# Two tuned MoE layers on one core: where finished sums are emptied, and a further block whose matmuls use 64-row tiles

## The chip, the cores and the metric

One core of a Trainium2 chip. The metric is the device time of one execution in microseconds (us): the median of three executions, beside one profiled execution whose trace is read here.

## What is computed

A causal 7-tap convolution with softmaxed weights of its own for every token, then two feed-forward layers of width 2048, each with its own activation:

```
w = softmax(weight_gen)                    # 8192 tokens, 8 heads, 7 taps
x = sum over k of w[..., k] * x_pad[t + k]  # 192 channels
h = x @ w_in;   g = h if h >= 1, 0 if h <= -1, else (h + 1)**2 / 4;   x = g @ w_out      # layer 1
h = x @ w_in2;  g = h - tanh(h);                                      out = g @ w_out2   # layer 2
```

## The kernel before, in words

**Blocks and items.** The 8192 tokens are 16 blocks of 512, the 2048 hidden units 16 groups of 128. An item (m, b, f) is layer m (0 and 1 in the code, layers 1 and 2 in the words), block b, group f. It has a first product into one PSUM bank (`ps6`, `ps7`, `ps1`, `ps0` in turn), an activation, and a second product that adds to the block's two sum banks (`ps2`, `ps3` in layer 1; `ps4`, `ps5` in layer 2 from block 1 on). Each float32 operand is split into a rounded part and a rest, and the products are taken of the parts. So an item has these operations between its two products: in layer 1 ACT L795 and L796, DVE L797, ACT L801 (`gh`, the rounded part), DVE L805 (`gl`, the rest); in layer 2 ACT L799, DVE L800, then L801 and L805 alike. `g` has 3 buffers, `gh` and `gl` have 4.

**Order of the blocks.** From the sixth block on layers take turns: layer 1 of block 3, layer 2 of block 2, layer 1 of block 4, layer 2 of block 3, and so on to layer 1 of block 15, layer 2 of block 14 and last layer 2 of block 15.

**Two modes of TensorE.** In 128-row mode (`mm1`, L781, and L817 to L824) an item is 5 + 5 matmuls of 512 columns, one after another. In 64-row mode two half-height matmuls run beside each other, the low lane and the high lane; the 192 inputs of a block then need no padding, and an item is 19 half-height matmuls, 9.5 for each lane. `paired(m, b)` (L641) says which blocks use it. There the plan takes two items f, f+1 as a pair of 19 steps, in three pieces (`both`, L720): `one` (9 steps), `two` and `three` (5 each). Piece `three` of a pair holds the low half of the second product of the even item of the pair before; piece `two` that of the odd item of two pairs before; high halves follow later. A sum is therefore complete only in the third pair of the next block (`done`, L714).

**Beside them.** The convolution of a later block: 0.95 us operations on DVE (L445, L492, L581, L576, L584), paced by `turn` (L385). It ends in two 32 by 32 transposes (L576) whose rows go to DRAM and come back as the next layer-1 block's input (`move_rows`, DMAs L596, L603 to L607). And the emptying of a finished sum: `finish1` (layer 1: ACT L856, DVE L858, ACT L853, DVE L857, ACT L859, DVE L860, and the copy `x3` L865 that 64-row mode needs) and `finish2` (layer 2: ACT L886, DVE L887, L888, L889, then 24 stores L884).

**What sets the order.** A list scheduler at build time (`Plan.run`): each task has a key, the item at which it is due, and each modelled engine takes the ready task with the smallest key. It only fixes the order in which each engine's instructions stand. On the chip each engine works its list in that order, and an instruction waits for the data it needs, holding up all behind it on its engine.

Of the kernel before, what the change touches and what calls it, by code (L numbers as in the profile page):

```python
# [23 lines left out]
MOVED = 4  # L24
# [133 lines left out]
def on(engine, dur):  # L158
    return {engine: (dur, 0.0)}
# [3 lines left out]
def tile_dynconv_moe_moe(  # L163
# [17 lines left out]
    NB = NT // N  # L181
    NF = FF // P
    D1 = D - P
# [46 lines left out]
    def x3(s):  # L230

        n, k = divmod(s.n, 2)
        if n not in x3_t:
            x3_t[n] = const.tile([P, 2, N], F32R, tag=f"raw{n}", name=f"x3_{n}")
        return x3_t[n][D1:P, k]
# [14 lines left out]
    plan = Plan()  # L250
# [23 lines left out]
    order = []  # L274
# [10 lines left out]
    marks = {}  # L285
# [81 lines left out]
    xdone = {}  # L367
    a_of, b_of, x3_of = {}, {}, {}
    x3_free = []

    def conv(b, banks, base, gap):
# [7 lines left out]
        count, paced = [0], [0.0]  # L379
# [5 lines left out]
        def turn(k):  # L385

            if b < MOVED:
                return []
            paced[0] += k
            n = int(base + PACE * paced[0])  # L390
            return [marks["gl", it] for it in [order[n]] if n < at[0, b, 0] and ("gl", it) in marks]

        def load_wg(e):
# [38 lines left out]
        t = plan.add(on("DVE", 0.30), key(), lambda e: e.tensor_reduce(MX(), W(), axis=AX.X, op=ALU.max), [lw] + turn(0.5), takes=soft, uses=[wg], own=0.12 if early else 0.0)  # L432
        t = plan.add(on("DVE", 0.30), key(), lambda e: e.tensor_tensor(W(), W(), bc(MX()), op=ALU.subtract), [t] + turn(0.5), uses=[wg] + soft, lock=not early)
# [51 lines left out]
        tasks, sums = [], []  # L485
# [152 lines left out]

    def paired(m, b):

        return b >= MOVED - m and (m, b) != (1, NB - 1)  # L641

    def lanes1(i):

# [69 lines left out]
    def done(g, t):  # L714

        if g in late2 and late2[g][2] == NF - 1:
            m, b, f, *_, acc, need = late2[g]
            (finish1 if m == 0 else finish2)(b, acc, g + (9.0 if m == 0 else 11.0), t)

    def both(m, b, f, h0, h1, need):  # L720

# [46 lines left out]
    def item(m, b, f, after):  # L768
# [36 lines left out]
        tlo = plan.add(engines, i, lambda e: e.tensor_tensor(GL(), G_(), GH().bitcast(F32), op=ALU.subtract), [thi], takes=[gl], uses=[g], lock=True)  # L805

        marks["gl", (m, b, f)] = tlo
        w = wout[m][:, f, :]
        a, z = f == 0, f == NF - 1
        need = [wdone.get((1, m, f // 2)), prev2.get((m, b))]  # L810
# [31 lines left out]
            (finish1 if m == 0 else finish2 if b < NB - 1 else finish_last)(b, acc, i + LAG + 0.6, t)  # L842
        return first

    def finish1(b, acc, key, t):
        s, tm = slot("xt"), slot("val")
        b_of[b] = s
        X, M = lambda k: xt_t[s.n][:, k], lambda: vals[tm.n][0:D1]
        p0, p1 = lambda: ps[acc[0].n], lambda: ps[acc[1].n]

        def hi(e):
            xt_tile(s, f"b_{b}")
            e.copy(X(0), p0())  # L853

        h0 = plan.add(on("ACT", 0.60), key, hi, [t], takes=[s], uses=acc)
        h1 = plan.add(on("ACT", 0.60), key, lambda e: e.copy(M(), p1()[D1:P]), [t], takes=[tm], uses=acc)  # L856
        l0 = plan.add(on("DVE", 0.60), key, lambda e: e.tensor_tensor(X(1), p0(), X(0).bitcast(F32), op=ALU.subtract), [h0], uses=acc + [s])  # L857
        r = plan.add(on("DVE", 0.60), key, lambda e: e.tensor_tensor(M(), p1()[0:D1], M(), op=ALU.add), [h1], uses=acc + [tm])  # L858
        rh = plan.add(on("ACT", 0.525), key, lambda e: e.copy(X(2)[0:D1], M()), [r], uses=[s, tm])  # L859
        rl = plan.add(on("DVE", 0.60), key, lambda e: e.tensor_tensor(X(2)[D1:P], M(), X(2)[0:D1].bitcast(F32), op=ALU.subtract), [rh], uses=[s, tm])  # L860
        marks["fin1", b] = r
        xdone[1, b] = [h0, l0, rh, rl]
        if paired(1, b):
            s3 = x3_of[1, b] = slot("x3")
            xdone[1, b].append(plan.add(on("ACT", 0.525), key, lambda e: e.copy(x3(s3), M()), [r] + x3_free, takes=[s3], uses=[tm]))  # L865

    def out_raws():

        return (0, 1)

    def finish2(b, acc, key, t):

        s, tm = slot("raw", out_raws), slot("val")
        R = lambda: raws[s.n].rearrange("p a b -> p (a b)").bitcast(F32)
        M = lambda: vals[tm.n][0:D1]
        p0, p1 = lambda: ps[acc[0].n], lambda: ps[acc[1].n]

        def store(e, c):
            r = R()[c * 32:(c + 1) * 32, 0:N] if c < P // 32 else R()[c * 32 - P:c * 32 - P + 32, N:]
            r = r.rearrange("p (u v c) -> p u v c", u=T, c=32)  # L880
            for n in range(T):

                o = out_sq[:, :, b * T + n, c * 32:(c + 1) * 32]
                e.dma_start(o, r[:, :, n] if b >= MOVED else r[:, n])  # L884

        h1 = plan.add(on("ACT", 0.60), key, lambda e: e.copy(M(), p1()[D1:P]), [t], takes=[tm], uses=acc)  # L886
        t0 = plan.add(on("DVE", 0.60), key, lambda e: e.transpose(R()[:, 0:N], p0()), [t], takes=[s], uses=acc)  # L887
        r = plan.add(on("DVE", 0.60), key, lambda e: e.tensor_tensor(M(), p1()[0:D1], M(), op=ALU.add), [h1], uses=acc + [tm])  # L888
        t1 = plan.add(on("DVE", 0.60), key, lambda e: e.transpose(R()[0:D1, N:], M()), [r, t0], uses=[s, tm])  # L889
        for c in range(D // 32):  # L890
            plan.add(on("DMA", 2.6), key, lambda e, c=c: store(e, c), [t0 if c < P // 32 else t1], uses=[s], late=3.0)

# [29 lines left out]
    for n, (m, b) in enumerate(streams):  # L922
# [5 lines left out]
        for f in range(NF):  # L928
# [9 lines left out]
            if (m, b, f) == (1, NB - 2, NF - 1):  # L938
                close(at[m, b, f] + 1)

    tasks = plan.run()
    with tc.manual_schedule():
        for t in tasks:
# [41 lines left out]
```

## Time and profile before

| | before |
|---|---|
| runs | 1181.68, 1182.35, 1183.67 us, median 1182.35 |
| the profiled execution | 1182.38 us, of which the span from first to last instruction is 1180.6 us |
| PE | 1144.8 us busy, 97% of the span |
| DVE, ACT, POOL | 995.9 (84%), 849.1 (72%), 94.0 us (8%) |
| granted TensorE clock | mean 0.995 of full speed; under nine tenths in the second of 40 slices alone |
| DMA | 60.5 MB, 51 GB/s over the span |

An engine's busy time is the union of its instructions. A matmul's end is modelled, so short gaps between matmuls hardly show in PE's busy time; the distance between the starts of two matmuls shows them.

### The profile page before, as it was taken

The page shows a single profiled execution, that of the slowest core. Times are in us where ns is not written, and L with a number is a line of the kernel's source. Part 1 is how long each engine was busy: PE and PEld are TensorE (multiplying, and loading weights), DVE is VectorE, ACT ScalarE, POOL GpSimd, SP SyncE. Part 2 cuts the span into 40 slices and gives each one's busy share as a digit, 9 for nine tenths or more (in the row PEclk, how much of TensorE's full clock was granted, in tenths as well). Part 3 has the DMA queues.
Part 4 walks back from the last instruction along what each step waited for, and adds up shares of the span by engine and source line. Part 5 has one row for each costly group of instructions (what it writes and reads, how often), then busy time and mean ns, then how long its engine had stood idle before and what let it go on. Part 6 is the DMA issues. An engine that isn't in the chain of part 4 may idle for free.

```text
span 1180.6 us, 23472 instructions
## 1 busy us (share of the span) xinstructions
PE 1144.8 (97%) x8648; PEld 1027.2 (87%) x8648; DVE 995.9 (84%) x1523; ACT 849.1 (72%) x1511; POOL 94.0 (8%) x81
## 2 busy tenths in 40 slices
PE   3899999999999999999999999999999999999998
PEld 2677888888998998889989888999989999999987
DVE  8998998887988879898888989889888888976665
ACT  4989996675867767677676867767686676767653
POOL 4744451000000000000000000000000000000000
PEclk9899999999999999999999999999999999999999
DMA  6522130211130301203021130301213020110000
GB/s 206 161 71 79 54 121 8 52 50 48 19 92 13 89 11 32 79 15 96 9 53 51 19 92 15 96 4 33 76 19 92 12 62 1 27 47 15 1 10 19
DMA packets 93034, 60.50 MB, mean 51 GB/s; under 512 B 56060, under 2 KB 81274, under 8 KB 92920
## 3 DMA queue, kind: packets, MB, share of 16 engines
q1 hardware_dynamic: 92732, 58.62, 18.1%
q8 instruction: 68, 1.11, 0.4%
q10 hardware_dynamic: 188, 0.39, 0.1%
q14 instruction: 46, 0.38, 0.1%
HBM read 43.24 MB, written 15.73 MB: 50 GB/s over the span
## 4 chain that ended last, share of the span: by engine, by line
PE 87%; ACT 6%; DVE 4%; issue 1%; POOL 1%; DMA 1%; DVEq 0%; ACTq 0%
PE ps L677 36%; PE ps L693 31%; PE ps L781 10%; PE ps L823 2%; PE ps L824 2%; PE ps L817 2%; PE ps L818 2%; PE ps L819 2%; ACT g L795 1%; ACT g L796 1%; ACT gh L801 1%; PE ps L834 1%; DVE gl L805 1%; DVE raw L887 1%; ACT val L886 1%
## 5 line engine op out<-in xcount | busy, mean ns | idle before, releaser
L677 PE MATMUL ps<-gh,wout 64*128 64x512 f32 x2304 | 731.9, 387 | 0.0
L677 PE MATMUL ps<-gl,wout 64*128 64x512 f32 x1536 | 597.8, 389 | 3.2 <-DVE gl L805 3.1
L677 PEld LDWEIGHTS ps<-gh,wout 64*128 64x128 f32 x2304 | 421.8, 184 | 26.4 <-ACT gh L801 0.3
L693 PE MATMUL ps<-a,win 64*128 64x512 f32 x1632 | 408.7, 389 | 0.0
L693 PE MATMUL ps<-b,win 64*128 64x512 f32 x1632 | 403.1, 387 | 0.0
L801 ACT CAST gh<-g 128x512 fp32r<-128x512 f32 x512 | 314.3, 617 | 105.1 <-PE ps L677 40.6
L805 DVE TENSOR_TENSOR gl<-g,gh 128x512 fp32r<-128x512 f32 x476 | 327.5, 692 | 41.4 <-ACT gh L801 26.2
L693 PEld LDWEIGHTS ps<-a,win 64*128 64x128 f32 x1632 | 298.1, 184 | 14.4 <-issue 0.4
L693 PEld LDWEIGHTS ps<-b,win 64*128 64x128 f32 x1632 | 300.2, 184 | 5.6
L677 PEld LDWEIGHTS ps<-gl,wout 64*128 64x128 f32 x1536 | 282.7, 184 | 19.7 <-DVE gl L805 12.1
L799 ACT ACTIVATE g<-ps 128x512 f32<-128x512 f32 x256 | 152.8, 598 | 132.6 <-PE ps L693 115.0
L800 DVE TENSOR_TENSOR g<-ps,g 128x512 f32<-128x512 f32 x256 | 174.0, 686 | 67.7 <-ACT g L799 66.5
L797 DVE SCALAR_TENSOR_TENSOR g<-ps,g 128x512 f32<-128x512 f32 x256 | 174.6, 685 | 47.5 <-ACT g L796 44.8
L795 ACT ACTIVATE g<-ps 128x512 f32<-128x512 f32 x256 | 151.5, 592 | 53.5 <-PE ps L693 38.7
L796 ACT ACTIVATE g<-g 128x512 f32<-128x512 f32 x256 | 161.9, 632 | 6.5
L781 PE MATMUL ps<-a,win 128*128 128x512 f32 x320 | 88.0, 411 | 6.2 <-POOL win L351 3.1
L781 PE MATMUL ps<-b,win 128*128 128x512 f32 x320 | 83.3, 391 | 0.0
L781 PEld LDWEIGHTS ps<-a,win 128*128 128x128 f32 x320 | 62.7, 198 | 23.4 <-POOL win L351 4.3
L445 DVE TENSOR_TENSOR prod<-xw,wg 128x768 f32<-128x768 f32 x84 | 80.9, 963 | 0.0
L693 PE MATMUL ps<-x,win 64*128 64x512 f32 x192 | 74.3, 387 | 0.0
L781 PEld LDWEIGHTS ps<-b,win 128*128 128x128 f32 x320 | 59.1, 188 | 12.0 <-issue 0.4
L492 DVE TENSOR_TENSOR acc<-acc,prod 128x768 f32<-128x768 f32 x70 | 67.4, 963 | 0.0
(89 smaller groups left out, 890.4 us busy)
## 6 DMA issues: line engine op xcount, KB each, us to landing
xw<-in_x_dram SPq DMA_DIRECT2D x14, 960.0 KB, 7.0
spot<-xw SPq DMA_DIRECT2D x96, 96.0 KB, 2.0
raw<-in_moe_w_out_dram SPq DMA_DIRECT2D x16, 384.0 KB, 3.1
a<-spot SPq DMA_DIRECT2D x24, 256.0 KB, 3.3
out_dram<-raw SPq DMA_DIRECT2D x360, 16.0 KB, 1.5
raw<-in_moe_w_in_dram SPq DMA_DIRECT2D x16, 256.0 KB, 3.4
raw<-in_moe_w_in_dram SPq DMA_DIRECT2D x32, 128.0 KB, 3.4
a<-spot SPq DMA_DIRECT2D x24, 128.0 KB, 3.3
```

The lines of the kernel that those rows point to most:

```text
L445: e.tensor_tensor(dst.rearrange("p j (h g) -> p j h g", h=H), xws[xw.n][:, k:k + T, :].rearrange("p j (h g) -> p j h g", h=H), w[:, :, :, ...
L492: e.tensor_tensor(prods[k % 2] if early and k == mine - 1 else acc_sb, acc_sb, prods[k % 2], op=ALU.add)
L677: return e.matmul(to(), w[rs, c:c + P], (GL() if low else GH())[rs], start=f == 0 and lane == 0 and n == 0, stop=f == NF - 1 and lane == 1 ...
L693: return e.matmul(ps[h.n], win[m][rs, k, fs], x, start=lane == 0 and n == 0, stop=lane == 1 and n == len(ops) - 1)
L781: e.matmul(ps[h.n], w[:, k, fs], xt[:, c], start=n == 0, stop=n == 4)
L795: t = plan.add(on("ACT", 0.60), i, lambda e: e.activation(G_(), H_(), AF.Relu, bias=0.5, scale=0.5), [first], takes=[g], uses=[h], late=0.1)
L796: t = plan.add(on("ACT", 0.537), i, lambda e: e.activation(G_(), G_(), AF.Square), [t], uses=[g])
L797: t = plan.add(on("DVE", 0.605), i, lambda e: e.scalar_tensor_tensor(G_(), H_(), 1.0, G_(), op0=ALU.max, op1=ALU.min), [t], uses=[g, h])
L799: t = plan.add(on("ACT", 0.49), i, lambda e: e.activation(G_(), H_(), AF.Tanh), [first], takes=[g], uses=[h])
L800: t = plan.add(on("DVE", 0.605), i, lambda e: e.tensor_tensor(G_(), H_(), G_(), op=ALU.subtract), [t], uses=[g, h])
L801: thi = plan.add(on("ACT", 0.527), i, lambda e: e.copy(GH(), G_()), [t], takes=[gh], uses=[g])
L805: tlo = plan.add(engines, i, lambda e: e.tensor_tensor(GL(), G_(), GH().bitcast(F32), op=ALU.subtract), [thi], takes=[gl], uses=[g], lock= ...
```

## The change

Three edits.

1. The emptying of a sum in 64-row mode gets dependences in the plan alone (`held`): each of its ACT and DVE operations stands behind `gh` or `gl` of a certain later item. If g is the last item of the block, so that g + 4 is f = 3 of the next block, then the copy of half a sum stands behind `gh` of f = 3, and the other operations behind `gh` or `gl` of f = 4, 5 and 6.
2. `turn` skips f = 3 to 6 when it paces the convolution of blocks 4 to 15.
3. `paired` takes in layer 2 of block 2: 16 more items in 64-row mode. Its block then needs an `x3` copy (13 of them now instead of 12), and this copy now reads the rounded part in `b` and not `val`.

```diff
-            paced[0] += k
-            n = int(base + PACE * paced[0])
+            paced[0] += k * PACE
+            while int(base + paced[0]) % NF in (3, 4, 5, 6):
+                paced[0] += 1.0
+            n = int(base + paced[0])
...
-        return b >= MOVED - m and (m, b) != (1, NB - 1)
+        return b >= MOVED - 2 * m and (m, b) != (1, NB - 1)
...
-            (finish1 if m == 0 else finish2)(b, acc, g + (9.0 if m == 0 else 11.0), t)
+            (finish1 if m == 0 else finish2)(b, acc, g + (9.0 if m == 0 else 11.0), t, g)
...
+    held = []
+    def hold(g, tasks):
+        if g is not None:
+            held.extend((t, kind, g + n) for t, kind, n in tasks)
...
+        hold(g, [(h1, "gh", 4), (r, "gl", 5), (h0, "gh", 5), (l0, "gl", 6), (rh, "gh", 6), (rl, "gl", 7)])
...
-            xdone[1, b].append(plan.add(on("ACT", 0.525), key, lambda e: e.copy(x3(s3), M()), [r] + x3_free, takes=[s3], uses=[tm]))
+            xdone[1, b].append(plan.add(on("ACT", 0.525), key, lambda e: e.copy(x3(s3), X(2)[0:D1]), [rh] + x3_free, takes=[s3], uses=[s]))
...
+        hold(g, [(h1, "gh", 4), (r, "gl", 5), (t0, "gl", 6), (t1, "gl", 7)])
...
+    for t, kind, n in held:
+        t.deps.append(marks[kind, order[n]])
```

In the changed kernel every line from L389 on stands 2 or more lines later: L797 is L799 there, L805 L807, L445 L447, L492 L494, L677 L679, L693 L695, L781 L783, and L887, L888, L889 are L898, L899, L900.

DVE, from the third item of a layer-1 block on (block 5; the same in blocks 4 to 14). `g` written from a `ps` bank is the activation of the next item (f = 2, 3, then 4, 5, 6, 7), `gl` the rest of the items in the same order, `raw` and `val` the emptying, `prod` and `acc` the convolution. Before:

```order
L797 SCALAR_TENSOR_TENSOR g2_97<-ps1_66,g2_97 128x512
L797 SCALAR_TENSOR_TENSOR g0_95<-ps0_65,g0_95 128x512
L887 STREAM_TRANSPOSE raw0_85<-ps4_64 128x512
L805 TENSOR_TENSOR gl0_102<-g2_97,gh3_101 128x512
L805 TENSOR_TENSOR gl2_104<-g0_95,gh0_98 128x512
L445 TENSOR_TENSOR prod0_94<-xw1_92,wg1_78 128x768
L797 SCALAR_TENSOR_TENSOR g1_96<-ps6_67,g1_96 128x512
L888 TENSOR_TENSOR val0_89<-ps4_64,val0_89 64x512
L889 STREAM_TRANSPOSE raw0_85<-val0_89 64x512
L805 TENSOR_TENSOR gl1_103<-g1_96,gh1_99 128x512
L797 SCALAR_TENSOR_TENSOR g2_97<-ps7_68,g2_97 128x512
L492 TENSOR_TENSOR acc0_93<-acc0_93,prod0_94 128x768
```

And in the change:

```order
L799 SCALAR_TENSOR_TENSOR g2_97<-ps1_66,g2_97 128x512
L799 SCALAR_TENSOR_TENSOR g0_95<-ps0_65,g0_95 128x512
L807 TENSOR_TENSOR gl0_102<-g2_97,gh3_101 128x512
L807 TENSOR_TENSOR gl2_104<-g0_95,gh0_98 128x512
L799 SCALAR_TENSOR_TENSOR g1_96<-ps6_67,g1_96 128x512
L799 SCALAR_TENSOR_TENSOR g2_97<-ps7_68,g2_97 128x512
L807 TENSOR_TENSOR gl1_103<-g1_96,gh1_99 128x512
L899 TENSOR_TENSOR val0_89<-ps4_64,val0_89 64x512
L807 TENSOR_TENSOR gl3_105<-g2_97,gh2_100 128x512
L898 STREAM_TRANSPOSE raw0_85<-ps4_64 128x512
L799 SCALAR_TENSOR_TENSOR g0_95<-ps1_66,g0_95 128x512
L799 SCALAR_TENSOR_TENSOR g1_96<-ps0_65,g1_96 128x512
```

Before, the transpose of the sum stood ahead of `gl` of f = 2 and 3, and convolution operations stood around the activations of f = 4 and 5; now the emptying stands behind `gl` of f = 4 and f = 5, and the next convolution operation comes behind `gl` of f = 7.

DVE, in the layer-2 block that follows (block 4), at the convolution's second transpose. Before, it stands between `gl` of f = 0 and f = 1's, here the last two rows:

```order
L800 TENSOR_TENSOR g2_97<-ps7_68,g2_97 128x512
L805 TENSOR_TENSOR gl1_103<-g1_96,gh1_99 128x512
L576 STREAM_TRANSPOSE xw1_92<-acc0_93 128x4x6x32
L805 TENSOR_TENSOR gl3_105<-g2_97,gh2_100 128x512
```

And in the change:

```order
L802 TENSOR_TENSOR g1_96<-ps1_66,g1_96 128x512
L802 TENSOR_TENSOR g2_97<-ps0_65,g2_97 128x512
L807 TENSOR_TENSOR gl0_102<-g1_96,gh3_101 128x512
L870 TENSOR_TENSOR b_4_3113<-val1_90,b_4_3113 64x512
L807 TENSOR_TENSOR gl2_104<-g2_97,gh0_98 128x512
L578 STREAM_TRANSPOSE xw1_92<-acc0_93 128x4x6x32
```

It has moved behind `gl` of f = 7 (the last `gl` row), past the emptying of layer 1's sum.

TensorE at the start of layer 2 of block 2. Before:

```order
L781 MATMUL ps6_67<-b_2_1217,win1_82 128x512 x5
L817 MATMUL ps2_63<-gh2_100,wout0_83 128x512
L818 MATMUL ps2_63<-gh2_100,wout0_83 128x512
L819 MATMUL ps2_63<-gh2_100,wout0_83 128x512
L823 MATMUL ps2_63<-gl3_105,wout0_83 128x512
```

And in the change:

```order
L695 MATMUL ps6_67<-b_2_1217,win1_82 128x512 x5
L695 MATMUL ps7_68<-b_2_1217,win1_82 128x512 x4
L679 MATMUL ps2_63<-gh2_100,wout0_83 128x512
L695 MATMUL ps6_67<-b_2_1217,win1_82 128x512
L679 MATMUL ps2_63<-gh2_100,wout0_83 128x512
```

Single matmuls of full height became interleaved half-height ones, one block earlier than before. Ahead of this place TensorE's and POOL's lists are the same in both kernels; behind layer 2 of block 2 TensorE's is the same again.

## Rows read from the trace of the kernel before

**Rows 1.** The page, part 1: busy time, share of the span, instructions.

```profile
PE 1144.8 (97%) x8648; PEld 1027.2 (87%) x8648; DVE 995.9 (84%) x1523; ACT 849.1 (72%) x1511; POOL 94.0 (8%) x81
```

**Rows 2.** Five blocks: stretch, length, then busy PE, PEld, DVE, ACT, POOL, clock, DMA.

```profile
217.75:254.02 36.27, 36.27 (x162) 30.04 (x160) 31.21 (x47) 27.29 (x49) 0.00 (x0) 1.00 0.08 15
254.02:290.38 36.36, 36.36 (x162) 29.86 (x160) 29.34 (x49) 22.73 (x39) 0.00 (x0) 1.00 0.24 75
...
360.61:396.14 35.53, 35.25 (x306) 31.65 (x305) 31.82 (x47) 27.75 (x48) 0.00 (x0) 1.00 0.09 16
396.14:430.81 34.67, 34.67 (x306) 34.05 (x305) 28.53 (x46) 22.50 (x40) 0.00 (x0) 1.00 0.27 78
1062.82:1097.48 34.66, 34.66 (x306) 33.98 (x305) 22.87 (x35) 27.57 (x48) 0.00 (x0) 1.00 0.08 13
```

**Rows 3.** Timeline of ACT: first activation of layer 1 in blocks 4, 5, 15.

```profile
293.77 0.60 ACT L795 ACTIVATE g<-ps 128x512 f32<-128x512 f32 x1 [2.28 <-PE ps L677]
...
364.10 0.60 ACT L795 ACTIVATE g<-ps 128x512 f32<-128x512 f32 x1 [1.03 <-PE ps L693]
...
1066.30 0.60 ACT L795 ACTIVATE g<-ps 128x512 f32<-128x512 f32 x1 [1.03 <-PE ps L693]
```

**Rows 4.** Waits of PEld from 290 to 1062 us: total, times, longest.

```profile
PEld ps L677 <- DVE gl L805: 12.1, 22, 0.7
```

**Rows 5.** Timeline, layer 1 of block 5, pair f = 4, 5: start, duration, engine.

```profile
370.09 1.42 DVE L797 SCALAR_TENSOR_TENSOR g<-ps,g 128x512 f32<-128x512 f32 x2
...
371.45 0.58 ACT L886 COPY val<-ps 64x512 f32<-64x512 f32 x1
...
372.06 0.72 DVE L887 STREAM_TRANSPOSE raw<-ps 128x512 f32<-128x512 f32 x1 [0.56 <-ACT val L886]
372.70 0.60 ACT L795 ACTIVATE g<-ps 128x512 f32<-128x512 f32 x1 [0.15 <-PE ps L693]
372.70 1.25 DVE L805 TENSOR_TENSOR gl<-g,gh 128x512 fp32r<-128x512 f32 x2
...
372.74 0.39 PE L693 MATMUL ps<-a,win 64*128 64x512 f32 x1
373.41 0.50 PE L677 MATMUL ps<-gl,wout 64*128 64x512 f32 x1 [0.28 <-DVE gl L805]
```

**Rows 6.** Length and DVE busy time by pair, block 5 (f = 4, 6, 8, 12).

```profile
369.27:374.22 4.95, 4.34 (x8) 1.00 0.04 8
374.22:378.59 4.37, 4.34 (x7) 1.00 0.20 32
378.59:383.12 4.53, 4.42 (x8) 1.00 0.21 33
...
387.46:391.80 4.34, 4.28 (x7) 1.00 0.01 4
```

**Rows 7.** Timeline of DVE and PEld up to the second stall of that block.

```profile
376.05 0.70 DVE L889 STREAM_TRANSPOSE raw<-val 64x512 f32<-64x512 f32 x1
...
379.32 0.94 DVE L445 TENSOR_TENSOR prod<-xw,wg 128x768 f32<-128x768 f32 x1
...
382.32 0.18 PEld L677 LDWEIGHTS ps<-gl,wout 64*128 64x128 f32 x1 [0.34 <-DVE gl L805]
```

**Rows 8.** Layer 2 of block 4: transpose, gl of f = 7, last move, landing.

```profile
402.75 0.97 DVE L576 STREAM_TRANSPOSE xw<-acc 128x768 f32<-128x768 f32 x1
...
415.98 0.69 DVE L805 TENSOR_TENSOR gl<-g,gh 128x512 fp32r<-128x512 f32 x1 [0.32 <-PE ps L677]
...
407.88 0.45 SPq L605 DMA_DIRECT2D a<-spot  x1
...
DMA to landing us min/median/max: 2.9/3.5/4.0
```

**Rows 9.** Groups of instructions: the copy for 64-row mode.

```profile
L865 ACT CAST x<-val 64x512 fp32r<-64x512 f32 x12 | 7.4, 620 | 0.3
```

**Rows 10.** Timeline of SP, layer 1 of block 5: the 24 stores.

```profile
372.81 12.34 SPq L884 DMA_DIRECT2D out_dram<-raw  x24
```

More of the change, by code (lines that the diff above doesn't have):

```diff
@@ L807, in item @@
         marks["gl", (m, b, f)] = tlo
+        marks["gh", (m, b, f)] = thi
         w = wout[m][:, f, :]
@@ L843, in item, with finish1 @@
         return first
-    def finish1(b, acc, key, t):
+    held = []
+    def hold(g, tasks):
+        if g is not None:
+            held.extend((t, kind, g + n) for t, kind, n in tasks)
+    def finish1(b, acc, key, t, g=None):
         s, tm = slot("xt"), slot("val")
@@ L864, in finish1, with finish2 @@
             s3 = x3_of[1, b] = slot("x3")
-            xdone[1, b].append(plan.add(on("ACT", 0.525), key, lambda e: e.copy(x3(s3), M()), [r] + x3_free, takes=[s3], uses=[tm]))
+            xdone[1, b].append(plan.add(on("ACT", 0.525), key, lambda e: e.copy(x3(s3), X(2)[0:D1]), [rh] + x3_free, takes=[s3], uses=[s]))
     def out_raws():
         return (0, 1)
-    def finish2(b, acc, key, t):
+    def finish2(b, acc, key, t, g=None):
         s, tm = slot("raw", out_raws), slot("val")
```

## The prediction

> **What bounds the kernel now.** I began with the busy times of the page: TensorE is busy 97% of the span, DVE 84%, ACT 72% [rows 1]. TensorE sets the time, so the question for every edit is whether TensorE has fewer steps to do, or waits less. The second view cuts the span into blocks. A layer-2 block in 64-row mode takes 34.67 us, in which TensorE is busy throughout [rows 2]. That is the pace of the mode: 16 items are 8 pairs of 19 steps, 152 steps, 0.228 us each; a pair takes 4.33 us. A layer-1 block has as many steps, and in block 15 it does take 34.66 us; in block 5 it takes 35.53 us [rows 2]. The two differ in one thing: beside block 15 no convolution runs. Its DVE is busy 22.87 us, block 5's 31.82 us.
>
> The waits say where the 0.87 us goes. From 290 to 1062 us the weight loads of the second product wait for `gl`, 22 times [rows 4]: twice in each of the eleven layer-1 blocks 4 to 14. The timeline shows the first one. TensorE wants `gl` of f = 2 one step behind 372.74, at 372.97, which is 3.70 us into the pair f = 4, 5 (it begins at 369.27); it gets on at 373.41 [rows 5]. DVE was late because it was emptying the last layer-2 block: its two L797 ended at 371.51, then it waited until ACT's copy L886 was over, did the transpose L887 from 372.06, and only then `gl`, from 372.70 on. The pair took 4.95 us instead of 4.33. In that pair and the next DVE is busy 4.34 of 4.95 and 4.34 of 4.37 us [rows 6]: it has L888, L889 and up to three convolution operations to do beside the four of the items, so it falls behind, a convolution operation at 379.32 comes before the next items, and `gl` of f = 6 is late too, until 382.32 [rows 7]. This second stall costs about 0.2 us: its pair takes 4.53 us [rows 6].
>
> **The change, part by part.** *Emptying behind later items, and no convolution beside it.* No operation of DVE is added or removed; they are moved. I walk through the pair where the stall was, on a clock without stalls, with 0 at the pair's start. An even item's first product is ready 3.49 us into its pair (first activation 364.10, block start 360.61 [rows 2, 3]), an odd one's one five-step piece later, 1.14 us. TensorE wants `gl` of an even item 3.70 us into the next pair; an odd item has longer. Operations in a row start 0.60 us apart on DVE (two L797 take 1.42, two L805 1.25 us [rows 5]), a 0.95 us convolution operation holds the next one 0.87 us.
>
> - f = 2: the transpose is gone from before it, so `gl` runs from 371.51 to about 372.2, with 0.75 us to spare. ACT's copy now follows `gh` of f = 3, at about 372.15 to 372.75; the next activation could not begin before 372.70 [rows 5], so ACT loses nothing.
> - f = 4: activation from 3.49, square to 4.73, L797 to 5.45; f = 5 the same to 6.65; then `gl` of f = 4 to 7.3. It is wanted at 4.33 + 3.70 = 8.03: 0.7 us to spare.
> - Then, in the new list, the sum L888 (7.2 to 7.9), `gl` of f = 5 (to 8.5) and the transpose (to 9.1). L797 of f = 6 can begin at 7.82 + 1.3 = 9.1. The emptying fits into the gap.
> - f = 6: its `gl` ends at 11.6 and is wanted at 12.36. Then the second transpose, `gl` of f = 7 and one convolution operation, which ends at 13.6; L797 of f = 8 could begin at 13.45.
>
> The fullest pairs of the new list hold four item operations and two of the convolution, 4 x 0.60 + 2 x 0.87 = 4.14 us of 4.33; before, the pair f = 4, 5 held six of 0.60 and two of 0.87, with a third of the latter behind it. A pair as full as 4.14 exists already, 387.46 to 391.80 us: busy 4.28 of 4.34 and not stretched [rows 6]. So I take both stalls as gone in all eleven blocks; their lists are alike.
>
> The price of them all: from the first activation of layer 1 in block 4 to that in block 15 are 772.53 us (1066.30 - 293.77 [rows 3]), eleven layer-1 and eleven layer-2 blocks. At 34.66 and 34.67 us they would take 762.63. **Saved: 9.9 us.**
>
> *What the moves push elsewhere.* The layer-2 block gets three convolution operations more, 2.7 us, and the emptying of layer 1 later. DVE has 28.53 us to do in 34.67 there [rows 2], and an item has one ACT operation less: nothing. ACT's cast between the convolution's operations now stands ahead of the tanh of f = 2 and may hold it some 0.5 us, out of 1.3 us of room (the 0.7 of above and the square of 0.63 us that layer 2 does not have): nothing. The 24 stores on SP (12.34 us from 372.81 [rows 10]) begin some 6 us later and end near 391, inside the same block, with no other job of SP due there but one load: nothing. The rows of the convolution start later; that has a margin, counted under the rivals.
>
> *Layer 2 of block 2 in 64-row mode.* 36.36 us in 128-row mode become 34.67 [rows 2]: 1.7 us. Entering the mode costs something, once, wherever it stands: the block before it ends 0.09 us long (36.36 against 36.27 [rows 2]), and the first pair I estimate at as much again, 0.2 in all, which the two figures above count as saved. **Saved: 1.5 us.** The added copy is 0.62 us of ACT [rows 9], well ahead of its use, in a layer-2 block, where ACT has over 10 us to spare [rows 2]: nothing. The copies that were there read `b` instead of `val` and wait for one more ACT operation; their block is next but one. The same kind of stall could come at the new entrance, out of layer 1 of block 3 with its convolution; there the items are further apart (2.27 us) and the last `gl` are ready in time.
>
> The sum: 1182.38 - 9.9 - 1.5 = **1171.0 us** for the profiled execution, which stands 0.03 us from the median of the three runs. With every stall gone, TensorE's own steps are what is late next in blocks 4 to 14, and the even items' `gl` with 0.6 to 0.75 us of room.
>
> **The rivals.** *Stalls stay or come back elsewhere.* The room is 0.6 us; an unseen delay of ACT or DVE of that size would bring back a stall in each layer-1 block. Priced by the smaller one that is there, 4.53 - 4.33 = 0.2 us x 11: 1173.2 us; by the larger one, 0.62 x 11: 1177.8 us. For it: pairs with two convolution operations are near full. Against it: such pairs run without a stall now.
>
> *DVE is the real bound of these blocks.* The moved work is the same work, and a block of 35.53 us with 31.82 us of DVE work would keep its length with the waits in other places. Then only block 2 gains: 1182.38 - 1.5 = 1180.9 us. Against it: 3.7 us of the block are free on DVE, over four times the stall, and the full pair of rows 6 was not stretched. The Trainium skill, TensorEngine Tiling (Array Packing), Performance Considerations, holds that tiling the array speeds up TensorE but not the emptying of PSUM, which may become the bottleneck. By that rule this rival would be the outcome. The blocks that are in this mode already show DVE short of full, so the trace does not bear it out as a matter of throughput. An order that did not reach the chip's waits at all would give the same 1180.9 us.
>
> *Slower: the moved rows come too late.* In block 4 the second transpose of the convolution ends at 403.72 and the last move of the rows is issued at 407.88 and lands within 4.0 us, at 411.9 [rows 8]: 8.2 us. In the new list the transpose stands behind `gl` of f = 7, which ended at 416.67 [rows 8]; it would end at 417.6, the rows land at 425.8. Layer 1 of the next block begins at 430.81 [rows 2]: 5.0 us of room. Were the way 14.2 us instead of 8.2, each of eleven layer-1 blocks would begin 1.0 us late, and all that is gained is lost; at 16 us the time is 1171.0 + 11 x 2.8 = 1202 us. Against it: nothing else is on SP's queue then, and the first half of the rows leaves earlier than that.
>
> **How the numbers follow.** Forecast 0.83, between 1169.5 and 1172.2 (the runs of before spread 2 us). Stalls that stay 0.11, more likely near the small price: 1173.2, to 1177.8. DVE as the bound, or an order without effect, 0.04: 1180.9. Rows too late 0.02: over 1182.4. The range that leaves out no more than 2 in 10 is 1169.5 to 1174.5. A difference under 0.2%, 2.4 us, could not be told from none. Faster by more: the first two, 0.94; within: 0.04; slower: 0.02.
>
> **What would show it.** Right: the 22 waits of `gl` between 290 and 1062 us gone; layer-1 blocks 34.7 us from first activation to first tanh; in block 5 the transpose L898 behind `gl` of f = 5; layer 2 of block 2 in 34.7 to 34.9 us; about 144 more matmuls, of half height. Wrong: `gl` waits of TensorE in other pairs (first rival), layer-1 blocks of 35.5 us with waits of another name (second), a wait for a DMA at the start of layer-1 blocks (third).

## The result, and the profile after

| | before | after |
|---|---|---|
| runs | 1181.68 to 1183.67 us, median 1182.16 (5 runs) | 1171.37, 1166.01, 1166.03, 1165.84, 1165.81 us, median 1166.01 |
| ratio, 95% interval | | 0.987 [0.9848, 0.9893] |
| the profiled execution | 1182.38 us | 1171.37 us, span 1169.6 us |

The changed kernel is 1.3% faster. An execution of it takes either about 1171.3 or about 1166.0 us: of 21 executions in five sessions ten took 1170.96 to 1171.52, eleven 1165.71 to 1166.12, and none a time between. The forecast was 1171.0: the profiled execution met it, and the four others of that session lie 5 us below it. So there are two results to read, the slower pace first.

The page of the profiled execution, busy times, answers to [rows 1]:

```profile
PE 1136.6 (97%) x8792; PEld 1067.7 (91%) x8792; DVE 991.9 (85%) x1523; ACT 857.5 (73%) x1512; POOL 94.4 (8%) x81
```

There are 144 more matmuls of half height and one ACT operation more. Four blocks (stretch, length, then busy PE, PEld, DVE, ACT, POOL, clock, DMA), to be held against [rows 2]: layer 2 of block 2, layer 1 of block 5, layer 2 of block 4, layer 1 of block 15.

```profile
254.38:289.14 34.76, 34.76 (x295) 32.25 (x296) 29.47 (x48) 21.59 (x37) 0.00 (x0) 1.00 0.28 82
358.48:393.14 34.66, 34.66 (x306) 33.98 (x305) 29.39 (x45) 27.82 (x48) 0.00 (x0) 1.00 0.08 13
393.14:427.81 34.67, 34.67 (x306) 33.99 (x305) 30.66 (x49) 23.14 (x40) 0.00 (x0) 1.00 0.27 82
1051.81:1086.48 34.67, 34.67 (x307) 34.00 (x305) 22.72 (x35) 27.57 (x48) 0.00 (x0) 1.00 0.08 13
```

Block 5 lost its 0.87 us: it is now as long as block 15, although DVE still does 29.39 us of work beside it. The 2.4 us of DVE work that left it stand partly in the layer-2 block behind (28.53 before, 30.66 now), which did not get longer. Block 2 went from 36.36 to 34.76. Before, the waits of PEld from 290 to 1062 us held 22 entries for `gl` [rows 4]; now the view of 254 to 1090 us has one line, at the entrance of the mode:

```profile
PEld ps L695 <- issue: 0.4, 1, 0.4
```

The timeline of DVE where the first stall was, pair f = 4, 5 of block 5, which now begins at 367.14 (start, duration):

```profile
369.33 1.48 DVE L807 TENSOR_TENSOR gl<-g,gh 128x512 fp32r<-128x512 f32 x2
372.02 0.69 DVE L799 SCALAR_TENSOR_TENSOR g<-ps,g 128x512 f32<-128x512 f32 x1 [1.20 <-ACT g L798]
373.17 0.69 DVE L799 SCALAR_TENSOR_TENSOR g<-ps,g 128x512 f32<-128x512 f32 x1 [0.46 <-ACT g L798]
373.77 0.68 DVE L807 TENSOR_TENSOR gl<-g,gh 128x512 fp32r<-128x512 f32 x1
374.37 0.68 DVE L899 TENSOR_TENSOR val<-ps,val 64x512 f32<-64x512 f32 x1
374.97 0.67 DVE L807 TENSOR_TENSOR gl<-g,gh 128x512 fp32r<-128x512 f32 x1
375.57 0.70 DVE L898 STREAM_TRANSPOSE raw<-ps 128x512 f32<-128x512 f32 x1
```

In [rows 5] both `gl` stood behind the transpose and began at 372.70, 3.43 us into the pair; now they begin 2.19 us into it. The rest is the list as the prediction walked through it, on its clock: `gl` of f = 4 ends at 7.31 (forecast 7.3), the sum at 7.91 (7.9), `gl` of f = 5 at 8.50 (8.5), the transpose at 9.13 (9.1).

The quicker pace has a profile too: a later execution of the same, unedited kernel (the fifteenth experiment), 1166.00 us. Its busy times, and its layer 1 of block 5 and layer 2 of block 4:

```profile
PE 1129.6 (97%) x8792; PEld 1053.2 (90%) x8792; DVE 993.2 (85%) x1523; ACT 859.3 (74%) x1512; POOL 94.3 (8%) x81
```

```profile
357.88:392.33 34.45, 34.45 (x307) 33.43 (x306) 29.44 (x45) 27.89 (x48) 0.00 (x0) 1.00 0.08 13
392.33:426.78 34.45, 34.45 (x306) 33.43 (x306) 30.68 (x50) 23.20 (x40) 0.00 (x0) 1.00 0.28 82
```

Here a block takes 34.45 us, a pair 4.307 instead of 4.333. Over the 200 pairs of the mode 0.0267 us each make 5.3 us, the whole difference between 1171.3 and 1166.0. It is not the clock, which was granted in full (1.00) in the blocks of both, and not the start, since layer 2 of block 2 begins at 254.38 us in the slower execution and at 254.42 in the quicker one. So 34.67 us, which the prediction took for the pace of the mode, had a loss in it, of which no view of waits has a line.

Where that loss lies shows in one pair of each. Matmuls of the slower execution, then weight loads behind the fence that they wait for (start, duration); gl, gh are the low lane's, b the high lane's:

```profile
603.64 0.39 PE L679 MATMUL ps<-gl,wout 64*128 64x512 f32 x1
603.69 0.39 PE L695 MATMUL ps<-b,win 64*128 64x512 f32 x1
603.86 0.40 PE L679 MATMUL ps<-gh,wout 64*128 64x512 f32 x1
603.92 0.38 PE L695 MATMUL ps<-b,win 64*128 64x512 f32 x1
604.10 0.39 PE L679 MATMUL ps<-gl,wout 64*128 64x512 f32 x1
...
604.33 0.39 PE L679 MATMUL ps<-gh,wout 64*128 64x512 f32 x1
...
604.57 0.39 PE L679 MATMUL ps<-gh,wout 64*128 64x512 f32 x1
```

```profile
603.73 0.18 PEld L679 LDWEIGHTS ps<-gh,wout 64*128 64x128 f32 x1
603.74 0.18 PEld L695 LDWEIGHTS ps<-b,win 64*128 64x128 f32 x1
```

The same place of the quicker execution:

```profile
601.54 0.39 PE L695 MATMUL ps<-b,win 64*128 64x512 f32 x1
601.60 0.39 PE L679 MATMUL ps<-gl,wout 64*128 64x512 f32 x1
601.77 0.39 PE L695 MATMUL ps<-b,win 64*128 64x512 f32 x1
601.82 0.39 PE L679 MATMUL ps<-gh,wout 64*128 64x512 f32 x1
...
602.05 0.39 PE L679 MATMUL ps<-gl,wout 64*128 64x512 f32 x1
...
602.28 0.39 PE L679 MATMUL ps<-gh,wout 64*128 64x512 f32 x1
...
602.50 0.39 PE L679 MATMUL ps<-gh,wout 64*128 64x512 f32 x1
```

```profile
601.64 0.18 PEld L679 LDWEIGHTS ps<-gh,wout 64*128 64x128 f32 x1
601.65 0.31 PEld L695 LDWEIGHTS ps<-b,win 64*128 64x128 f32 x2
```

Two things differ. In the slower execution the low lane's step starts 0.06 us ahead of the high lane's that stands behind it in the program; in the quicker one the high lane is ahead by as much: the lanes don't run in step, each works its own steps. And a step that orders the lanes (they add to the same bank) comes late in one: the low lane's `gh` step waits, through an instruction of POOL (`relay`), for the last old step of the high lane. Its weight load otherwise starts 0.22 us ahead of its matmul (223 ns); it starts 0.13 us ahead in the slower execution (603.73, 603.86), where the high lane is behind, and 0.18 us ahead in the quicker one (601.64, 601.82). Behind it the low lane's matmuls in the slower execution stand up to 0.24 us apart for the rest of the pair (603.86 to 604.57: 0.71 for three), in the quicker one 0.227 (601.82 to 602.50: 0.68).

### The profile page after: what moved, and what is told of

The parts are those of the page before. It is cut to its first block, busy times and chain, and to the rows that moved or that the text cites. A ratio compares the mean times of both kernels' runs of the same rounds, so it can differ in the third digit from the quotient of the medians.

```text
span 1169.6 us, 23895 instructions
## 1 busy us (share of the span) xinstructions
PE 1136.6 (97%) x8792; PEld 1067.7 (91%) x8792; DVE 991.9 (85%) x1523; ACT 857.5 (73%) x1512; POOL 94.4 (8%) x81
## 4 chain that ended last, share of the span: by engine, by line
PE 91%; ACT 4%; DVE 2%; POOL 1%; issue 1%; DMA 1%; DVEq 0%; SPq 0%; ACTq 0%; POOLq 0%
PE ps L679 40%; PE ps L695 34%; PE ps L783 8%; PE ps L826 1%; PE ps L827 1%; PE ps L820 1%; PE ps L821 1%; PE ps L822 1%; PE ps L837 1%; ACT g L797 1%; ACT gh L803 1%; ACT g L798 1%; DMA wg<-in_weight_gen_dram 1%; PE ps L838 0%; ACT raw L322 0%
## 5 line engine op out<-in xcount | busy, mean ns | idle before, releaser
L679 PE MATMUL ps<-gh,wout 64*128 64x512 f32 x2400 | 760.1, 387 | 0.0
L679 PE MATMUL ps<-gl,wout 64*128 64x512 f32 x1600 | 619.7, 387 | 0.0
L679 PEld LDWEIGHTS ps<-gh,wout 64*128 64x128 f32 x2400 | 439.4, 184 | 16.8
L695 PE MATMUL ps<-b,win 64*128 64x512 f32 x1768 | 436.4, 387 | 0.0
L695 PE MATMUL ps<-a,win 64*128 64x512 f32 x1632 | 403.1, 387 | 0.0
L807 DVE TENSOR_TENSOR gl<-g,gh 128x512 fp32r<-128x512 f32 x476 | 328.9, 692 | 33.0 <-ACT gh L803 20.5
L695 PEld LDWEIGHTS ps<-b,win 64*128 64x128 f32 x1768 | 324.9, 184 | 1.3 <-issue 0.4
L695 PEld LDWEIGHTS ps<-a,win 64*128 64x128 f32 x1632 | 300.2, 184 | 0.0
L679 PEld LDWEIGHTS ps<-gl,wout 64*128 64x128 f32 x1600 | 294.7, 184 | 1.3
L799 DVE SCALAR_TENSOR_TENSOR g<-ps,g 128x512 f32<-128x512 f32 x256 | 175.0, 686 | 66.6 <-ACT g L798 63.5
L797 ACT ACTIVATE g<-ps 128x512 f32<-128x512 f32 x256 | 151.2, 590 | 54.6 <-PE ps L695 44.5
L783 PE MATMUL ps<-a,win 128*128 128x512 f32 x320 | 86.8, 406 | 6.3 <-POOL win L351 3.0
L783 PEld LDWEIGHTS ps<-a,win 128*128 128x128 f32 x320 | 61.4, 194 | 24.0 <-POOL win L351 4.1
L447 DVE TENSOR_TENSOR prod<-xw,wg 128x768 f32<-128x768 f32 x84 | 80.8, 962 | 0.0
L695 PE MATMUL ps<-x,win 64*128 64x512 f32 x200 | 77.2, 386 | 0.0
L494 DVE TENSOR_TENSOR acc<-acc,prod 128x768 f32<-128x768 f32 x70 | 67.6, 966 | 0.0
L783 PE MATMUL ps<-b,win 128*128 128x512 f32 x240 | 62.5, 392 | 0.0
L807 POOL TENSOR_TENSOR gl<-g,gh 128x512 fp32r<-128x512 f32 x36 | 51.4, 1434 | 53.8 <-ACT gh L803 37.3
```

Source lines behind the costliest of these rows:

```text
L447: e.tensor_tensor(dst.rearrange("p j (h g) -> p j h g", h=H), xws[xw.n][:, k:k + T, :].rearrange("p j (h g) -> p j h g", h=H), w[:, :, :, ...
L494: e.tensor_tensor(prods[k % 2] if early and k == mine - 1 else acc_sb, acc_sb, prods[k % 2], op=ALU.add)
L679: return e.matmul(to(), w[rs, c:c + P], (GL() if low else GH())[rs], start=f == 0 and lane == 0 and n == 0, stop=f == NF - 1 and lane == 1 ...
L695: return e.matmul(ps[h.n], win[m][rs, k, fs], x, start=lane == 0 and n == 0, stop=lane == 1 and n == len(ops) - 1)
L783: e.matmul(ps[h.n], w[:, k, fs], xt[:, c], start=n == 0, stop=n == 4)
L797: t = plan.add(on("ACT", 0.60), i, lambda e: e.activation(G_(), H_(), AF.Relu, bias=0.5, scale=0.5), [first], takes=[g], uses=[h], late=0.1)
```

## The experiments

Some expectations name theories. As I went on, A was: the 4.333 us hold a loss at the relay, and the emptying's stalls are a loss beside it. Each experiment's difference is against the changed kernel unless it says otherwise; the session's kernel before took 1182.65 us (experiments 1 to 4), 1182.72 (5 to 8), 1182.46 (9 to 12), 1182.1 (13 to 15).

**1 and 7. The changed kernel again**, unedited, in two other sessions.

> The changed kernel once more, nothing edited. Its profiled execution took 1171.4 us, the other four 1165.8 to 1166.0, all at a full clock. Theory A (two paces of the 64-row stream): a pair of items takes either 4.333 us, as in the profiled execution (19 steps of 0.2267 us and 0.027 us more), or 4.307 us (19 steps and nothing more), for all of the 200 pairs from 254 us on: 200 x 0.027 = 5.3 us. A profile of a 1166 us execution then has pairs of 4.307 us and its block 3 begins at the same 218 us. Theory B (the start): pairs take 4.333 us in both, and block 3 begins 5.3 us earlier in the short ones. Theory C (clock): all stages are 0.45% shorter alike.

> The changed kernel unedited, for whether executions of 1166 us come again. If they belong to a chip or to how the two lanes first meet, all executions here are alike: either 1171.4 us with pairs of 4.333 us or 1166.0 us with pairs of 4.307 us (theory A), or 1166.0 us with pairs of 4.333 us and a start 5.3 us shorter (theory B).

Measured: 1171.39 us (1171.20 to 1171.47), ratio 0.9904 [0.9891, 0.9918], and 1171.23 (1170.96 to 1171.39), 0.9901 [0.9886, 0.9916]. All eight executions lie near 1171.3, and in the two with a trace the pairs behind the entrance take 4.333 us. So the first session's 1166 was not the rule, and the profile of either pace could not be had at will.

**2. Block 2 in 128-row mode** again, the other two edits kept.

```diff
-        return b >= MOVED - 2 * m and (m, b) != (1, NB - 1)
+        return b >= MOVED - m and (m, b) != (1, NB - 1)
```

> The emptying behind later items and the pacing of the convolution, but layer 2 of block 2 in 128-row mode as before. By the sum of the prediction 1182.4 - 9.9 = 1172.5 us at the slower pace of pairs (4.333 us) and no pair of block 4 to 14 over 4.4 us. By theory A 192 pairs can also run at 4.307 us: 1167.4 us, and single executions lie at one of these two values. By theory B there may be any value between.

Measured: 1172.81 us (1172.58 to 1173.05), 1.42 more than experiment 1; no `gl` wait, and none of the four executions at the 1167.4 us that theory A allowed. The third edit is worth 1.4 us at this pace, the first two 9.8 (1182.65 - 1172.81); the prediction had 1.5 and 9.9.

**3. Block 2 alone.** No item is passed to `finish1` and `finish2`, so nothing is held, and `turn` paces as before.

```diff
-            (finish1 if m == 0 else finish2)(b, acc, g + (9.0 if m == 0 else 11.0), t, g)
+            (finish1 if m == 0 else finish2)(b, acc, g + (9.0 if m == 0 else 11.0), t)
```

> Layer 2 of block 2 in 64-row mode alone, the emptying and the pacing as in the kernel before. By the sum of the prediction 1182.4 - 1.5 = 1180.9 us, with the 22 waits for gl in layer-1 blocks as before, 4.95 and 4.55 us pairs among them. Theory A: a stall puts the two lanes of TensorE back into the slower pace, so no execution is 5 us shorter. Theory B: executions some 5 us shorter may occur here too (1175.6).

Measured: 1181.48 us (1180.67 to 1182.32), ratio 0.9988 [0.998, 0.9997]: 1.2 us less than before, and the 22 waits are back, 11.9 us in all. The two parts add up. None of the eleven executions was 5 us shorter, as theory A had it.

**4. Emptying held, convolution paced as before.**

```diff
-            paced[0] += k * PACE
-            while int(base + paced[0]) % NF in (3, 4, 5, 6):
-                paced[0] += 1.0
-            n = int(base + paced[0])
+            paced[0] += k
+            n = int(base + PACE * paced[0])
```

> Emptying behind later items and block 2 in 64-row mode, but the convolution paced as before, so that its operations stay among the items 4 to 7. If the place of the emptying alone matters, no stalls: 1171.0 us (or 1166). My theory is that DVE must also be given room: six operations of 0.60 us and two or three of 0.87 us in the pairs f = 6 to 9 are 5.3 us or more for 4.33, so a stall of 0.2 to 0.9 us stays in each of eleven blocks: 1173 to 1181 us, with waits for gl later than in the kernel before (f = 8 to 11).

Measured: 1172.11 us (1172.07 to 1172.57), ratio 0.9912 [0.9896, 0.9927], 0.7 more than with the pacing. I had expected the convolution to bring stalls of 0.2 us and more back. It did not; block 5 is 0.09 us longer, with DVE as busy as before the change [rows 2]:

```profile
358.64:393.39 34.75, 34.75 (x307) 33.81 (x305) 31.68 (x47) 27.92 (x48) 0.00 (x0) 1.00 0.09 16
```

**8. Convolution paced, emptying not held** (the edit of experiment 3 alone).

> Block 2 in 64-row mode and the convolution kept out of f = 3 to 6, the emptying where it was. The transpose of the sum still stands ahead of gl of f = 2, so the first stall stays: 0.62 us in each of eleven blocks; the second, which comes of the overload of DVE, should be gone, since the pair f = 4, 5 has six operations of 0.60 us and none of the convolution: 1171.4 + 11 x 0.62 = 1178 us. If only the place of the emptying mattered, both stalls would stay: 1181 us.

Measured: 1178.26 us (1177.93 to 1179.48), ratio 0.9963 [0.9948, 0.9977]. The first stall stays, once in each of the eleven blocks, and the second is gone:

```profile
PEld ps L679 <- DVE gl L807: 7.9, 11, 0.8
```

The two stalls thus have two causes, as the prediction said: the first is the transpose ahead of `gl`, the second the convolution on top of it. Holding the emptying takes away both (but for the 0.09 us of experiment 4), pacing the second alone, so their gains overlap: each edit taken alone with block 2's gives 10.5 and 4.5 us, both together 11.3.

**5. The relay with more room.** Piece `two` of a pair takes the first two `gh` steps of the even item before the odd item's two steps that wait for the relay, so these come two steps later. The same products are summed, in another order.

```diff
-            low = second(0, 0, g0, P_KINDS) + second(0, 1, g0, Q_KINDS)
+            low = second(0, 0, g0, P_KINDS) + second(0, 0, g1, P_KINDS)[:2]
...
-            weave(e, low, high, {(0, 0): "a", (0, 3): "b", (1, n): "a"}, {(1, 0): "b"} if n else {})
+            weave(e, low, high, {(0, 0): "a", (1, n): "a"}, {(1, 0): "b"} if n else {})
...
-            low = second(0, 0, g1, P_KINDS) + second(0, 1, g1, Q_KINDS)
+            low = second(0, 1, g0, Q_KINDS) + second(0, 0, g1, P_KINDS)[2:] + second(0, 1, g1, Q_KINDS)
...
-            weave(e, low, high, {(1, 0): "b"}, {(0, 2): "p", (0, 4): "q"})
+            weave(e, low, high, {(0, 0): "b", (1, 0): "b"}, {(0, 2): "p", (0, 4): "q"})
```

> The changed kernel with the low lane's steps of a pair in another order: the two gh steps of the even item (sum bank P) stand ahead of the odd item's two Q steps, so that the wait of the low lane for the high lane's last Q step, relayed through POOL, has 5 steps of room and not 3. Nothing is left out. In the trace of the changed kernel this relay ends about 0.05 us before the low lane's weight load starts, 0.09 us later than the other weight loads start, and the steps behind it take 0.230 to 0.236 us in place of 0.2267, in all 0.027 us in a pair. Theory A (this wait is what separates 4.333 from 4.307 us): pairs of 4.307 us throughout, 1171.4 - 200 x 0.027 = 1166.1 us. Theory B (the difference of 5.3 us lies elsewhere): 1171.4 us, pairs of 4.333 us.

Measured: 1166.1 us (1165.97 to 1166.3) in all four executions, ratio 0.9858 [0.9843, 0.9873], in the session in which the unedited kernel (experiment 7) took 1171.2 four times of four. Block 5, then layer 2 of block 4:

```profile
357.85:392.31 34.46, 34.46 (x307) 34.12 (x306) 29.44 (x45) 27.89 (x48) 0.00 (x0) 1.00 0.08 13
392.31:426.76 34.45, 34.45 (x306) 34.11 (x306) 30.66 (x50) 23.20 (x40) 0.00 (x0) 1.00 0.27 82
```

The load that waits for the relay now starts 0.22 us ahead of its matmul, like the others:

```profile
606.34 0.18 PEld L679 LDWEIGHTS ps<-gh,wout 64*128 64x128 f32 x1
606.56 0.39 PE L679 MATMUL ps<-gh,wout 64*128 64x512 f32 x1
```

This is the version that I would keep. The 5.3 us are to be had without a change to DVE or ACT: in the traces their instructions stand in the same order as in the changed kernel. By itself the run does not tell the room from a lucky entrance, since here too the high lane is 0.057 us ahead, as in the quicker unedited execution; experiments 9 and 12 do.

**6. Each relay made of two instructions of POOL**, otherwise the changed kernel.

```diff
         r = nc.gpsimd.nop(nofuse=True)
         tc.add_manual_dep(r.ins, q.ins.name, SYNC)
-        return r
+        r2 = nc.gpsimd.nop(nofuse=True)
+        tc.add_manual_dep(r2.ins, r.ins.name, SYNC)
+        return r2
```

> The changed kernel with each relay made of two POOL instructions, one waiting for the other: each relay some 0.06 to 0.1 us later, nothing else. Theory A: the relays with 3 steps of room are the ones that bind, so pairs get longer by up to two such hops, 4.39 to 4.53 us, 1183 to 1211 us. Theory B: relays have room, the time stays at 1171.4 us.

Measured: 1186.2 us (1185.93 to 1186.46), ratio 1.0029 [1.0018, 1.0039]. The second instruction starts 0.095 us behind the first; the weight load now starts 0.05 us ahead of its matmul, and a pair takes 4.407 us. Block 5:

```profile
359.92:395.17 35.25, 35.25 (x306) 30.55 (x305) 29.44 (x45) 27.82 (x48) 0.00 (x0) 1.00 0.08 13
```

So the relay has no spare room in this kernel: 0.095 us more of it cost 0.073 us a pair, 15 us in all, and again no view of waits names it.

**9. The kernel before, with the order of experiment 5.**

> The kernel before the change (no hold, no pacing, block 2 in 128-row mode) with the order of second products that let the fifth experiment run at 4.307 us a pair. Theory A (two separate losses in the kernel before: the stalls by gl, and 0.027 us in every pair by the late relay): the stalls stay as long as they are (first pair 4.9 to 5.0 us, second 4.5 to 4.6), the other pairs, some 150 to 170 of 192, take 4.307 us; 1182.5 less 4.0 to 4.5 gives 1178.0 to 1178.5 us; up to 1180.2 if the layer-1 blocks give their part back to DVE. Theory B (the quicker pair comes only where nothing stalls): 1182.5 us.

Measured: 1174.18 us (1173.87 to 1174.44), ratio 0.993 [0.9916, 0.9945]; 4 us less than theory A gave. The unstalled pairs do take 4.307 us, at other distances of the lanes than experiment 5's (the high lane 0.017 us behind). But the stalls shrank as well, which I had not expected: with other dependences the plan also put the transpose of the sum behind `gl` of f = 2, and the waits fell from 12.1 us [rows 4] to

```profile
PEld ps L677 <- ACT gh L802: 4.9, 13, 0.4
PEld ps L677 <- DVE gl L806: 3.6, 11, 0.4
```

So this run shows that the pace does not depend on the held emptying, nor on the high lane being ahead; as a measure of the loss at the relay, it is confounded.

**10. The changed kernel once more.**

> The changed kernel once more, unedited. Theory A (an execution either has every pair at 4.333 us or every pair at 4.307): either 1171.2 to 1171.5 us, pairs of 4.333, as in eight executions so far, or 1165.8 to 1166.0 us, and then the profile has pairs of 4.307 us and the low lane's weight load behind the relay no later than 190 ns ahead of its matmul. Theory B (the 5.3 us lie in another place): 1166 us with pairs of 4.333 us and a shorter head or tail.

Measured: 1171.52, 1166.12, 1165.89, 1166.00 us, median 1166.06, ratio 0.9873 [0.9851, 0.9895]. Both paces in one session; the execution with a trace was the one of 1171.52, with pairs of 4.333 us as in experiments 1 and 7.

**11. Experiment 5's order with experiment 6's relays.**

> The fifth experiment's order with every relay doubled, as in the sixth. There the second hop came 0.095 us behind the first, and a pair took 4.407 us. Theory A (only a relay without room costs anything): the relay in the middle has two steps more, so only those at the pair's start come late, by about 0.13 us: 4.33 to 4.35 us a pair, 1171 to 1175 us. Theory B (the two lanes run slower for each relay that they pass): 4.40 us a pair, 1185 us.

Measured: 1166.42 to 1166.74 us in three executions and 1172.62 in the profiled one, where pairs of 4.307, 4.333 and 4.353 us take turns. Theory B falls: eight relay instructions a pair instead of four cost next to nothing in themselves (1166.4 to 1166.7 us, where experiment 5 took 1166.0 to 1166.3). Theory A gave the profiled execution and missed the other three, which lie below its range. With late relays there are two paces again.

**12. Experiment 5's order, emptying held, convolution not paced.**

> The fifth experiment's order with the emptying held, but the convolution's pacing as before the change. Theory A (the pacing is worth little once the emptying is held; 0.7 us at 4.333 us a pair): layer-1 blocks 34.5 to 34.6 us, 1166.5 to 1168 us in all. Theory B (a quicker pair takes the room that made the pacing dispensable): stalls of 0.1 to 0.3 us come back in blocks 4 to 14, 1168 to 1171 us.

Measured: 1170.36 us (1170.1 to 1170.63), ratio 0.9899 [0.9882, 0.9915]. Theory B by the time: stalls come back in each layer-1 block, of 0.37 us in block 5, somewhat more than forecast:

```profile
358.24:393.07 34.83, 34.83 (x307) 33.02 (x305) 31.76 (x47) 27.96 (x48) 0.00 (x0) 1.00 0.09 16
```

The waits of PEld from 254 to 1090 us:

```profile
PEld ps L677 <- ACT gh L802: 3.3, 11, 0.3
PEld ps L677 <- DVE gl L806: 2.4, 11, 0.2
```

So the pacing, worth 0.7 us at 4.333 us a pair, is worth 4.3 (1170.36 against experiment 5's 1166.1, in another session) with this order at 4.307. Two things take the room, and the run does not separate them: the items come sooner, and the order itself wants the even item's `gh` two steps, 0.45 us, sooner. The longer of the two waits in block 5 is for this `gh`.

**13 and 14. Kicks.** In the first pair of a block the relay for the low lane (13: mark "b") or for the high lane (14: "p") gets 0 to 5 instructions more.

```diff
+            kick[0] = (2 * b + m) % 6 if f == 0 else 0
...
-                        fence[marks_at[lane, n]] = relay(q)
+                        fence[marks_at[lane, n]] = relay(q, 1 + kick[0] * (marks_at[lane, n] == "b"))
```

> The changed kernel, in which the relay that the low lane waits for in the middle of a pair has 0 to 5 hops more (2b+m modulo 6), in the first pair of each block alone. Each hop is 0.095 us, so each block begins with another distance between the lanes, and 7 untouched pairs follow. Theory A (the distance at which the lanes meet decides the pace): behind some kicks the pairs take 4.307 us for the rest of the block, behind others 4.333; the kicks themselves cost up to 0.45 us in each of 25 blocks, so 1171 to 1177 us in all. Theory B (the distance does not matter; something else decides, the same for a whole execution): 4.333 us in every untouched pair of the profile, 1176 to 1178 us.

> The same with the relay that the high lane waits for at the start of a pair; the kicked wait is then in the second pair of a block. Theory A: other distances, again some blocks at 4.307 us a pair and some at 4.333; 1171 to 1177 us. Theory B: 4.333 us in every untouched pair, 1176 to 1178 us.

Measured: 1175.24 us (1174.98 to 1176.68) and 1173.99 (1173.98 to 1174.64). Behind the kicks of 13 the high lane settles 0.063 or 0.003 us behind the low one, and the untouched pairs take 4.333 us. Behind those of 14 it settles 0.077 behind, and they take 4.327, a third pace (block 6: 34.61 us). So the pace does change with how the lanes stand to each other, which B denied. But A's forecast of 4.307 behind some kick was not met either: no kick left the high lane ahead for the pairs that follow.

**15. The changed kernel beside the two.**

> The changed kernel unedited, beside the two. Profile: 1171.2 to 1171.5 us. The others: 1166.0 us or 1171.3 us, as on the earlier chips. Theory A says that a small difference at the entrance of the mode picks one pace for the rest, so there may be both, and nothing between them.

Measured: 1165.98 us (1165.71 to 1166.05), ratio 0.9864 [0.985, 0.9879], four executions of four, and this time with a trace, shown above. The traces of the two paces differ from the entrance on. Both enter block 2 alike (the first pair takes 4.46 us), and the high lane then comes out 0.057 us ahead in the quicker one, 0.050 ahead in the slower one. At 0.057 the pairs take 4.307 us, and the distance stays. At 0.050 the low lane's next pairs take 4.333 us, but the high lane's 4.347, 4.367 and 4.360, so that its lead shrinks to 0.037 and 0.003 us and is lost; then the low lane leads, by 0.050 or 0.057 us in turn, for the rest, in pairs of 4.333.

## Why the prediction was right and wrong

**The step that failed** is this: "A layer-2 block in 64-row mode takes 34.67 us, in which TensorE is busy throughout. That is the pace of the mode: 16 items are 8 pairs of 19 steps, 152 steps, 0.228 us each; a pair takes 4.33 us", and what was built on it, "With every stall gone, TensorE's own steps are what is late next". TensorE's own steps take 19 x 0.2267 = 4.307 us; the remaining 0.027 us were lost at the relay between the lanes. The kernel before had them in all its pairs too (none in its trace is shorter than 4.333), also in the layer-2 blocks from which the pace was read, so the comparison of blocks could not show them. That PE was busy 34.67 of 34.67 us was no evidence: a matmul's modelled end fills such gaps, as the part on time and profile says. The distance of matmul starts held the answer. In layer 2 of block 4 before, the load behind the relay and its matmul stand 0.12 us apart, and the low lane's next steps 0.23 to 0.24:

```profile
411.74 0.18 PEld L677 LDWEIGHTS ps<-gh,wout 64*128 64x128 f32 x1
411.86 0.39 PE L677 MATMUL ps<-gh,wout 64*128 64x512 f32 x1
412.10 0.39 PE L677 MATMUL ps<-gl,wout 64*128 64x512 f32 x1
412.33 0.39 PE L677 MATMUL ps<-gh,wout 64*128 64x512 f32 x1
```

And 128-row mode would have given the unit: 36.27 us for 160 steps [rows 2] are 0.2267 each. No rival named it, and the range ended above 1166. Where 1171.0 was met, in the profiled execution and in all of experiments 1 and 7, it was by luck in this step: the executions fell on the pace in which the loss stays.

**Right, at the pace it assumed:** every other term. All 22 waits are gone; the layer-1 blocks are as long as the layer-2 blocks; 9.9 + 1.5 us were forecast and 1182.38 - 1171.37 = 11.0 measured between the two profiled executions. Experiments 2 to 4 give the parts: 9.8 for the first two edits, 1.2 to 1.4 for block 2, and 10.5 for block 2 and the held emptying. The forecast list of DVE came to within 0.03 us at the four places compared above. The rows of the convolution are in time: no layer-1 block begins with a wait, although the second transpose starts 21.2 us into its block (at 414.30) instead of 6.6 [rows 2, 8].

**The rivals.** Stalls elsewhere: none at this pace; experiment 12 shows that it was near, for with pairs 0.026 us shorter, `gh` wanted sooner and no pacing they come. DVE as the bound of these blocks: fell, since a layer-1 block takes 34.45 us with 29.4 us of DVE work, and 34.75 with 31.7 (experiment 4). What the Trainium skill says in TensorEngine Tiling (Array Packing), Performance Considerations, that the copy out of PSUM may become the bottleneck (it says so of a fourfold speedup; here two lanes share the array), did not come about as a matter of amount: DVE does nearly the work of before, 31.7 us, in a block of 34.75 (experiment 4). What emptying cost was its place ahead of `gl`, 0.62 us a block, and 0.2 more with the convolution on top of it. Late rows: fell. An order without effect: fell.

**What stays open.** Shown are: two paces of one program, the distance of the lanes at each, a late weight load where the pace is slow, a longer pair where the relay is made longer (experiment 6), and that room at the relay gives 4.307 us at every distance seen: the high lane 0.057 us ahead in experiment 5, and 0.017 to 0.063 behind in 9 and 12, where only pairs at a stall or within a few pairs of one take longer. With the high lane 0.063 us behind, a pair takes 4.307 us with the room (experiment 12) and 4.333 without it (the kernel before, experiment 13). Not shown is how a late load slows the steps behind it. Lateness alone does not decide: 0.04 us late costs nothing with the high lane 0.057 us ahead and 0.027 a pair in the low lane, 0.040 in the high one, with it 0.050 ahead, and in the quicker executions the high lane's first load of each pair comes 0.09 us late at no cost. Nor is it known what makes the 7 ns at the entrance; within a session most executions, but not always the traced one, fall alike. Nor is it shown why the quicker pace came with the change: no execution of the kernel before took under 1181.18 us, and none of experiment 3, which has the same stalls, under 1180.67. In the trace before, the lanes stand anew behind each stall and the high lane is never 0.057 us ahead, so the stalls may have kept the pace away.

## What to carry to other kernels

Work that is due soon for nobody (emptying a sum, a side computation) costs by its place in the list of an engine with room: put it behind the operation that the bounding engine waits for, and check that the new list keeps a gap there. Before taking the best stretch of a profile for the pace of the hardware, divide it by its steps and compare with the unit in another stretch: a loss that every stretch has shows in no comparison and, where ends are modelled, in no busy time. Where two streams are ordered through a third engine, give the hand-over several steps of room, or it can set the pace.

## What the runs showed of the hardware

- Two lanes of 64 rows run independently: a step of the high lane starts 0.057 us before the one that stands ahead of it in the program, and stays there for 200 pairs. Where they are ordered only by semaphores, either can lead.
- A hand-over from one lane to the other through POOL takes 0.49 us from the start of the marking step to the start of the waiting weight load (603.24 to 603.73), over two steps, though the instruction on POOL takes 17 ns; each further one adds 0.095 us.
- A weight load of the mode starts 0.22 us ahead of its matmul and takes 0.18. One that came 0.09 us late did not delay its own matmul, but at some distances of the lanes the steps behind it stretched to 0.23 to 0.24 us, which is in no view of waits.
